# Packed attention into a gated feed-forward: token halves on the partition halves, batch 0 turned by TensorE, attention matmuls beside `pp @ w`, three output buffers

## The chip, the cores and the metric

The kernel runs on one core of a Trainium2 chip. The metric is the device time of one launch in microseconds, from the first to the last instruction of the core with what the launch adds around it. Three runs of the kernel before took 767.19, 770.46 and 770.11 us, a median of 770.11 us. The engines that matter are TensorE (PE; its weight loads are counted apart as PEld), VectorE (DVE), ScalarE (ACT), GpSimd (POOL) and the queue of SyncE (SP), which issues nearly all DMAs.

## What is computed

```python
def sm_attn(qq, kk, vv):                       # softmax attention, scale 1/8
    a = exp(s - max(s)); a = a / (sum(a) + 1e-9)   # s = scale * qq @ kk.T
    return a @ vv
p_packed = sm_attn(p, k, v)                    # 32 packed queries look at 576 tokens
out = sm_attn(q, p_packed, p_packed)           # 576 tokens look at the 32 packed rows
x = out.transpose(0, 2, 1, 3).reshape(8 * 576, 512)
return (x @ w_a) * (x @ w_b) @ w_out           # 512 -> 1536 -> 512
```

There are 8 batches, 8 heads, 576 tokens, a head size of 64 and 32 packed rows. q, k, v and p are float32; the three weight matrices come in as float64 (18.9 MB in all) and are turned into float32 on the chip.

## The kernel before

**The algebra.** `x` is never built. For a batch and a head, `x` is `a2 @ pp`, where `pp` is the packed result (32 rows of 64) and `a2` the second softmax (576 x 32). So `x @ w = a2 @ (pp @ w)`, and with 8 heads of 32 rows the inner dimension is 256, as two tiles of 128. The kernel computes `g = pp @ w` in pieces (`g_tiles`, line 276 on), then `g` times `a2` (`mm1`, `mm1_half`), multiplies the two branches, and multiplies by `w_out` (`mm2_part`). To keep float32 accuracy in fp32r matmuls, operands are split into a high and a low part, and each product is three matmuls (high by high, high by low, low by high).

**A batch on TensorE.** There are 12 steps `ft` of `mm1`, each of two halves of 12 matmuls 128 x 288 (line 303), then the output tiles of `mm2`, each 36 matmuls 128 x 512 (line 329): four tiles after an even batch and five after an odd one. `g_tiles` gives two steps' worth at a time (16 records at line 284, tiles of 64 x 32 of the array), six times a batch; one of the six stands ahead of the last `mm2` tile of the batch before.

**The attention of the next batch** lies between those matmuls. `stage1(b, e)` makes the first softmax of four heads: eight scores matmuls (line 201), maximum and exp, five transposes of `a1` (lines 224 and 225), then 20 small matmuls by v (line 234), scaled into `pp`. `stage2(b, u)` makes the second softmax of one token half: eight matmuls (line 250), a 32 x 32 transpose, maximum, subtraction, exp, sum, scaling, transpose back, and the high and low parts `a2_hi` and `a2_lo`. `turned` transposes p and `pp` on TensorE (line 190) into `pT` and `ppT`. Both stages are generators: each `next` runs one step up to a `yield`.

**What sets the order.** All engines are scheduled by hand. Two strings, `FIRST` and `START`, give the order of loads and of batch 0's attention and weight conversions before the main loop. `PLAN` (and `PLAN_0` during batch 0) says at which slot which step of the next batch is emitted. There is a slot after each half of `mm1` (0 to 23) and after each three `ft` of an `mm2` tile (24 on). `g_tiles` is emitted after slots 1, 5, 9, 13 and 17. In the strings `S` and `r` are steps of stage 1, `s` of stage 2, `T` and `P` the two `turned`, `k` and `q` the turning of loaded k and q, `L..` loads, `g` the first `g_tiles`, and `A`, `B`, `C`, `D` the conversion of one weight piece (high word on ACT, low word on ACT, DVE or POOL, joined on DVE, and for `w_out` the split on ACT and POOL). There are 36 pieces in 12 raw buffers; a new load waits until a `C` has freed one.

**q and k before the change.** Tokens lie along the free dimension and head parity on the two partition halves: rows 64e to 64e+63 hold the 64 features of head 2r+e. `load` (line 107) reads 128-byte runs, eight DMAs of 72 KB for half of a batch's k or q, so that VectorE's 32 x 32 transposes (line 117) finish the turning. In `stage1` all eight scores matmuls of one `e` read the same partition half: two token halves one behind the other on the same 64 rows of the array. In `stage2` both partition halves are used at a time.

**PSUM.** Three pools: `ps_m` (two buffers of two banks: `mm1`, `mm2`), `ps_s` (one of two banks: scores) and `ps_x` (two banks: `g`, transposes, the product with v). An output tile goes through one SBUF buffer `ob`, which also takes each converted `w_out` piece.

Of the kernel before, what the change touches and what calls it, by code (L numbers as in the profile page):

```python
# [19 lines left out]
def tile_packed_attn_gated_ffn(  # L20
# [78 lines left out]
    def load(src, key, b, i, engines=(nc.sync,)):  # L99

        pool = scratch if b == 0 and key == "q" else ld
        t = pool.tile([P, 2, TX, TL], F32, name=f"nat{i}")
        for r in range(2):
            for e in range(E):
                for w in range(2):
                    g = 64 * e + 32 * w
                    engines[w % len(engines)].dma_start(  # L107
                        out=t[g:g + TL, r],
                        in_=src[b, 2 * (2 * i + r) + e, :, TL * w:TL * w + TL].rearrange("(x l) d -> l x d", l=TL))
# [12 lines left out]
    def load_v(b, e):
        t = ld.tile([P, R, NT, D], F32, name="vt") if b or e == 0 else scratch.tile([P, R, NT, D], F32, name="vt1")
        vv = v[b].rearrange("(r e) s d -> e s r d", e=E)[e]
        nc.sync.dma_start(
            out=t[:, :, 0:4, :], in_=vv[0:512].rearrange("(p i) r d -> p r i d", i=4))
# [60 lines left out]
    def turned(dst, src):  # L187

        tp = bank()
        nc.tensor.transpose(tp[:, 0:P], src.rearrange("p e d -> p (e d)"), ident)  # L190
# [4 lines left out]
    def stage1(b, e):  # L195

        rows = slice(64 * e, 64 * e + 64)
        s = bank_pair(b or e == 0)
        for half in range(2):
            for r in range(R):  # L200
                nc.tensor.matmul(  # L201
                    out=s[J * r:J * r + J, half, 0:HS], lhsT=pT[rows, r, :],
                    rhs=xT_cols(b, "k", rows, r, half), start=True, stop=True)
# [13 lines left out]
        a1v = a1[:, 0:512].rearrange("p (t i) -> p i t", i=4)  # L217
        if b == 0 and e:
            pair = bank_pair()
# [3 lines left out]
        for i in range(4):  # L223
            nc.tensor.transpose(tp[:, P * i:P * i + P], a1v[:, i, :], ident)  # L224
# [323 lines left out]
```

## Time and profile before

| | |
|---|---|
| median of three runs | 770.11 us |
| profiled execution | 769.02 us, its span 767.2 us |
| PE busy | 730.9 us (95% of the span) |
| PE in the first 40 us | 14.3 us |
| DVE, ACT, POOL busy | 309.1, 276.6, 205.6 us |
| first `mm1` matmul | at 43.96 us |
| first `mm1` matmul of batch 1 | at 137.60 us |
| first `mm1` matmul of batch 4 | at 411.92 us |
| DMA | 58.03 MB in 180,173 packets, 159,504 of them under 512 B |

The profile gives for each engine the time in which it executed something, in total and in 40 slices; a chain of waits, followed back from the last instruction; groups of instructions by source line; and a timeline by engine. In a timeline row stand the start, the duration, the engine, the source line, the operation with its output and input, and how many instructions were merged. Matmuls overlap, so what a piece of work costs on TensorE is read from the start of its first row to the start of the next piece, and not from its duration.

### The profile page before, as it was taken

The page shows a single profiled execution, that of the slowest core. Times are in us where ns is not written, and L with a number is a line of the kernel's source. Part 1 is how long each engine was busy: PE and PEld are TensorE (multiplying, and loading weights), DVE is VectorE, ACT ScalarE, POOL GpSimd, SP SyncE. Part 2 cuts the span into 40 slices and gives each one's busy share as a digit, 9 for nine tenths or more (in the row PEclk, how much of TensorE's full clock was granted, in tenths as well). Part 3 has the DMA queues.
Part 4 walks back from the last instruction along what each step waited for, and adds up shares of the span by engine and source line. Part 5 has one row for each costly group of instructions (what it writes and reads, how often), then busy time and mean ns, then how long its engine had stood idle before and what let it go on. Part 6 is the DMA issues. An engine that isn't in the chain of part 4 may idle for free.

```text
span 767.2 us, 13460 instructions
## 1 busy us (share of the span) xinstructions
PE 730.9 (95%) x5652; PEld 595.2 (78%) x5652; DVE 309.1 (40%) x482; ACT 276.6 (36%) x487; POOL 205.6 (27%) x151
## 2 busy tenths in 40 slices
PE   1569999999999999999999999999999999999998
PEld 0267777788778888788787887788888788788887
DVE  3589854544405443344504344054420544223200
ACT  2477653543214432244202542144311443224300
POOL 1154654223202241023401233022310224113300
PEclk9979999999999999999999999999999999999999
DMA  9899843423004230234002350043201310100001
GB/s 224 226 316 290 264 102 68 94 64 63 27 28 80 75 51 28 57 69 93 15 28 63 62 94 15 28 80 87 39 28 41 64 32 1 41 15 2 1 27 42
DMA packets 180173, 58.03 MB, mean 76 GB/s; under 512 B 159504, under 2 KB 167952, under 8 KB 180112
## 3 DMA queue, kind: packets, MB, share of 16 engines
q1 hardware_dynamic: 175376, 56.58, 30.0%
q10 hardware_dynamic: 4736, 0.59, 0.5%
q8 instruction: 44, 0.72, 0.4%
q14 instruction: 17, 0.14, 0.1%
HBM read 47.71 MB, written 9.44 MB: 74 GB/s over the span
## 4 chain that ended last, share of the span: by engine, by line
PE 91%; SPq 2%; DVE 2%; DMA 2%; issue 1%; POOL 1%; ACT 1%; DVEq 0%; ACTq 0%; POOLq 0%
PE m L303 40%; PE m L329 39%; PE x L284 6%; PE s L201 2%; SPq L107 2%; PE x L234 1%; PE s L250 1%; PE x L224 1%; DMA nat<-in_k_dram 1%; DMA vt<-in_v_dram 1%; POOL wo L83 1%; POOL h_lo L83 1%; DVE ob L156 0%; DMA nat<-in_q_dram 0%; ACT h_hi L322 0%
## 5 line engine op out<-in xcount | busy, mean ns | idle before, releaser
L329 PE MATMUL m<-wo,h_hi 128*128 128x512 f32 (+1 forms) x888 | 270.6, 387 | 1.7 <-ACT ob L342 1.5
L83 POOL TENSOR_TENSOR h_lo<-asb,h_hi 128x576 fp32r<-128x576 f32 x96 | 138.9, 1447 | 441.8 <-ACT h_hi L322 441.8
L329 PEld LDWEIGHTS m<-wo,h_hi 128*128 128x128 f32 x888 | 162.9, 188 | 46.0 <-ACT ob L342 7.9
L303 PE MATMUL m<-a_hi,ghi 128*128 128x288 f32 x768 | 175.4, 309 | 8.5 <-ACT a_hi L271 8.1
L329 PE MATMUL m<-wo,h_lo 128*128 128x512 f32 (+1 forms) x444 | 170.5, 384 | 0.0
L303 PE MATMUL m<-a_lo,ghi 128*128 128x288 f32 x768 | 164.8, 295 | 0.6 <-DVE a_lo L83 0.6
L303 PEld LDWEIGHTS m<-a_hi,ghi 128*128 128x128 f32 x768 | 121.9, 189 | 52.3 <-issue 34.3
L303 PE MATMUL m<-a_hi,glo 128*128 128x288 f32 x768 | 134.2, 296 | 0.1
L322 ACT CAST h_hi<-asb 128x576 fp32r<-128x576 f32 x96 | 64.8, 675 | 169.6 <-DVE asb L318 169.6
L303 PEld LDWEIGHTS m<-a_lo,ghi 128*128 128x128 f32 x768 | 125.2, 190 | 0.9 <-DVE a_lo L83 0.9
L318 DVE TENSOR_TENSOR asb<-m,asb 128x576 f32<-128x576 f32 x96 | 72.5, 756 | 125.5 <-PE m L303 118.3
L83 DVE TENSOR_TENSOR glo<-x,ghi 128x512 fp32r<-128x512 f32 x96 | 61.7, 684 | 131.4 <-ACT ghi L290 131.3
L303 PEld LDWEIGHTS m<-a_hi,glo 128*128 128x128 f32 x768 | 113.5, 189 | 0.3 <-DVE glo L83 0.3
L329 PEld LDWEIGHTS m<-wo,h_lo 128*128 128x128 f32 x444 | 83.5, 188 | 16.9
L342 ACT COPY ob<-m 128x512 f32<-128x512 f32 x35 | 20.6, 588 | 174.3 <-PE m L329 171.8
L315 ACT COPY asb<-m 128x576 f32<-128x576 f32 x96 | 61.6, 641 | 23.8 <-PE m L303 21.4
L284 PE MATMUL x<-w_ab,ppT 64*32 64x512 f32 x768 | 53.8, 609 | 0.0
L290 ACT CAST ghi<-x 128x512 fp32r<-128x512 f32 x96 | 51.3, 586 | 2.9 <-PE x L284 2.9
L117 DVE STREAM_TRANSPOSE xT<-nat 128x1152 f32<-128x1152 f32 x32 | 43.8, 1370 | 14.4 <-DMA nat<-in_k_dram 10.2
L145 ACT ACTIVATE raw<-raw 128x512 f32<-128x512 f32 x36 | 23.6, 678 | 15.8 <-DMA raw<-in_moe_w_a_dram 12.1
L201 PE MATMUL s<-xT,pT 64*32 64x288 f32 x240 | 19.7, 427 | 7.2 <-DVE pT L191 7.0
L261 ACT ACTIVATE t<-t 128x576 f32<-128x576 f32 x14 | 9.6, 686 | 43.2 <-POOL t L259 43.2
(86 smaller groups left out, 367.2 us busy)
## 6 DMA issues: line engine op xcount, KB each, us to landing
nat<-in_q_dram SPq DMA_DIRECT2D x128, 72.0 KB
nat<-in_k_dram SPq DMA_DIRECT2D x120, 72.0 KB
vt<-in_v_dram SPq DMA_DIRECT2D x16, 512.0 KB
out_dram<-ob SPq DMA_DIRECT2D x31, 256.0 KB
raw<-in_moe_w_a_dram SPq DMA_DIRECT2D x12, 512.0 KB
raw<-in_moe_w_b_dram SPq DMA_DIRECT2D x12, 512.0 KB
raw<-in_moe_w_out_dram SPq DMA_DIRECT2D x12, 512.0 KB
out_dram<-ob SPq DMA_DIRECT2D x10, 128.0 KB
```

Of the source, the lines that this page charges most:

```text
L83: return eng.tensor_tensor(out=dst, in0=src, in1=hi.bitcast(F32), op=ALU.subtract)
L117: nc.vector.transpose(out=xT.rearrange("p r t -> p (r t)"), in_=t.rearrange("p r x d -> p (r x d)"))
L145: nc.scalar.activation(out=high, in_=high, func=AF.Prelu, scale=2.0 ** -112, alpha=-2.0 ** 32)
L201: nc.tensor.matmul(out=s[J * r:J * r + J, half, 0:HS], lhsT=pT[rows, r, :], rhs=xT_cols(b, "k", rows, r, half), start=True, stop=True)
L284: nc.tensor.matmul(out=gps[e][J * r:J * r + J, :], lhsT=ppT[rows, b % 2, r, :], rhs=w_ab[rows, c, r, :], start=True, stop=True)
L290: nc.scalar.copy(out=ghi[:, e], in_=gps[e])
L303: nc.tensor.matmul(out=ps[:, half, 0:HS], lhsT=gt[:, kt, i, :], rhs=at[:, kt, HS * half:HS * half + HS], start=(n == 0), stop=(n == len(st ...
L315: nc.scalar.copy(out=asb, in_=pa[:, :, 0:HS])
L318: nc.vector.tensor_tensor(out=asb, in0=pb[:, :, 0:HS], in1=asb, op=ALU.mult)
L322: nc.scalar.copy(out=hh, in_=flat)
L329: nc.tensor.matmul(out=o[:, cols], lhsT=ht[:, c0:c0 + P], rhs=wt[:, cols], start=(ft == 0 and n == 0), stop=(ft == NFT - 1 and n == 2))
L342: nc.scalar.copy(out=ob, in_=o)
```

## The change

**Layout.** Half of the tokens now lies on each partition half, with all heads along the free dimension: rows 64u to 64u+63 hold the 64 features of token half u. For k the halves are even and odd tokens, for q alternating blocks of 32 tokens. A load of a half batch is four DMAs of 144 KB instead of eight of 72 KB. `stage1` takes one matmul of 288 columns on one partition half and, on the other, 256 and 32 columns (shifted, so that five contiguous chunks of `a1` match v's token order). `stage2(b, e)` now goes by head parity. Because both partition halves need every head of p and `pp`, both are transposed twice, with the two parities exchanged (`turned`, two transposes instead of one; `p_nat` and `pp` have a third column block that repeats the first).

**Batch 0** is loaded by `load_first` in 1 KB runs (512 B for the last 64 tokens), three DMAs each for k and q, and turned by 24 TensorE transposes each (`turn_first`), whose results ACT and DVE copy to `xT`. Its output rows come in another order and are stored in groups of 32 (`store_first`).

**Order.** `FIRST` puts p, k, q and v ahead of all weights; `START`, `PLAN` and `PLAN_0` are new. `stage1` and `stage2` yield once more, right behind their scores matmuls, so that these can be placed alone. `g` of the next batch is a task of the plan now. The product with v and the transposes of `a1` go to `ps_s` from batch 1 on. **Output tiles** go through three buffers (the two of `asb` and one that was named `ob`).

```diff
-    def load(src, key, b, i, engines=(nc.sync,)):
+    def load(src, key, b, i):
+        t = ld.tile([P, R, XH, TL], F32, name=f"nat{i}")
+        rows = src[b, R * i:R * i + R].rearrange("h s d -> (h s) d")
+        rows = rows.rearrange("(y l u) d -> u l y d" if key == "k" else "(y u l) d -> u l y d", u=2, l=TL)
+        for u in range(2):
+            for w in range(2):
+                g = 64 * u + 32 * w
+                nc.sync.dma_start(out=t[g:g + TL].rearrange("l h x d -> l (h x) d"), in_=rows[u][:, :, TL * w:TL * w + TL])
+    def load_first(src, key, part):
+        if part < 2:
+            t = scratch.tile([P, R, 4 * D], F32, name=f"{key}n{part}")
+            nc.sync.dma_start(out=t, in_=src[0, R * part:R * part + R, 0:4 * P, :].rearrange("h (p i) d -> p h (i d)", i=4))
+        else:
+            t = scratch.tile([P, H, 2 * D], F32, name=f"{key}n{part}")
+            nc.sync.dma_start(out=t[0:TR], in_=src[0, :, 4 * P:S, :].rearrange("h (p u) d -> p h (u d)", u=2))
+    def turn_first(key, n):
+        copy = (nc.vector.tensor_copy, nc.scalar.copy)[int(TURN["kq".index(key) * 5 + n])]
+        x = bank_pair()[:, 0, :] if n in (2, 3) else bank()
+        if n < 4:
+            h = 2 * (n % 2)
+            for i in range(4):
+                nc.tensor.transpose(x[:, P * i:P * i + P], firsts[key, n // 2][:, h + i // 2, P * (i % 2):P * (i % 2) + P], ident)
+            copy(out=xTs[0, key][n // 2][:, h:h + 2, 0:2 * P], in_=x.rearrange("p (h t) -> p h t", h=2))
+            return
+        for h in range(H):
+            nc.tensor.transpose(x[:, TR * h:TR * h + TR], firsts[key, 2][0:TR, h, :], ident[0:TR, 0:TR])
...
-        for half in range(2):
+        parts = [(0, 0, 0, HS), (1, TR, 0, 2 * P), (1, 0, 2 * P, TR)]
+        for u, c, t, n in parts:
             for r in range(R):
                 nc.tensor.matmul(
-                    out=s[J * r:J * r + J, half, 0:HS], lhsT=pT[rows, r, :],
-                    rhs=xT_cols(b, "k", rows, r, half), start=True, stop=True)
+                    out=s[J * r:J * r + J, u, c:c + n], lhsT=pT[64 * u:64 * u + 64, u ^ e, r, :],
+                    rhs=xT_cols(b, "k", u, 2 * r + e, slice(t, t + n)), start=True, stop=True)
+        yield
...
+        for i in range(2):
+            nc.tensor.transpose(tp[:, P * i:P * i + P], cols[:, 64 * (i ^ back):64 * (i ^ back) + P], ident)
...
+    def out_tile(i):
+        if i % 3 == 1:
+            return sm.tile([P, DO], F32, name="wo_f32", bufs=1)
+        return sm.tile([P, 2, HS], F32, name="asb").rearrange("p u t -> p (u t)")[:, 0:DO]
...
-    FIRST = ("p0 w1 k0 k1 w1 v0 w1 v1 w1 q0 q1 w1 w1 w1 w1 w1 w1 w1 w1")
+    FIRST = ("p0 k0 k1 k2 q2 q0 v0 q1 v1 w1 w1 w1 w1 w1 w1 w1 w1 w1 w1 w1")
```

**Where it moves instructions.** First the DMA queue of SP at the program's start (`nat` is a loaded k or q half, `kn` and `qn` the new ones, `raw` a weight piece; before, eight more DMAs of k go through ACT's queue, and eight more of q follow the last row). Before:

```order
L133 DMA p_nat<-in_p_dram 128x1x64 x2
L166 DMA raw<-in_moe_w_a_dram 128x2x512
L107 DMA nat_102<-in_k_dram 32x18x32 x4
L107 DMA nat_111<-in_k_dram 32x18x32 x4
L166 DMA raw<-in_moe_w_a_dram 128x2x512
L125 DMA vt<-in_v_dram 128x4x256
L127 DMA vt<-in_v_dram 64x4x64
L166 DMA raw<-in_moe_w_b_dram 128x2x512
L125 DMA vt_127<-in_v_dram 128x4x256
L127 DMA vt_127<-in_v_dram 64x4x64
L166 DMA raw<-in_moe_w_b_dram 128x2x512
L107 DMA nat_132<-in_q_dram 32x18x32 x8
```

With the change:

```order
L177 DMA p_nat<-in_p_dram 128x1x64 x3
L130 DMA kn_101<-in_k_dram 128x4x256
L130 DMA kn_103<-in_k_dram 128x4x256
L134 DMA kn_105<-in_k_dram 32x8x128
L134 DMA qn_107<-in_q_dram 32x8x128
L130 DMA qn_109<-in_q_dram 128x4x256
L165 DMA vt<-in_v_dram 128x4x256
L169 DMA vt<-in_v_dram 32x4x64 x2
L130 DMA qn_115<-in_q_dram 128x4x256
L165 DMA vt_117<-in_v_dram 128x4x256
L169 DMA vt_117<-in_v_dram 32x4x64 x2
L210 DMA raw<-in_moe_w_a_dram 128x2x512 x2
```

The 32 DMAs of k and q became six, and the first weight piece moved from the second place to behind all of k, q and v.

Then TensorE in `mm1`, around the scores of stage 1 (`s<-xT,pT`) and the second `g_tiles` (`x<-w_ab,ppT`) of a batch. Before:

```order
L303 MATMUL m<-a_hi,glo 128x288 x4
L201 MATMUL s<-xT_1451,pT 32x288 x2
L201 MATMUL s<-xT_1469,pT 32x288 x2
L201 MATMUL s<-xT_1451,pT 32x288 x2
L201 MATMUL s<-xT_1469,pT 32x288 x2
L303 MATMUL m<-a_hi,ghi 128x288 x2
```

With the change:

```order
L351 MATMUL m<-a_hi,glo 128x288 x4
L247 MATMUL s<-xT_1413,pT 32x288 x2
L247 MATMUL s<-xT_1423,pT 32x288 x2
L247 MATMUL s<-xT_1413,pT 32x256 x2
L247 MATMUL s<-xT_1423,pT 32x256 x2
L247 MATMUL s<-xT_1413,pT 32x32 x2
L247 MATMUL s<-xT_1423,pT 32x32 x2
L332 MATMUL x<-w_ab,ppT 32x512 x8
L351 MATMUL m<-a_hi,ghi 128x288 x2
```

The scores, which stood alone between two halves of `mm1`, stand right ahead of `g_tiles` now, and have twelve matmuls in place of eight.

Last, TensorE from the end of `mm1` into the first `mm2` tile, around stage 2's matmuls (`xT,ppT`). Before (a second group like the one shown stands three `ft` further on, and `g_tiles` ahead of the last tile):

```order
L303 MATMUL m<-a_hi,glo 128x288 x4
L329 MATMUL m<-wo,h_hi_396 128x512 x2
L329 MATMUL m<-wo,h_lo_397 128x512
L329 MATMUL m<-wo,h_hi_398 128x512 x2
L329 MATMUL m<-wo,h_lo_399 128x512
L329 MATMUL m<-wo,h_hi_400 128x512 x2
L329 MATMUL m<-wo,h_lo_401 128x512
L250 MATMUL s<-xT_1828,ppT 32x288 x4
L250 MATMUL s<-xT_1880,ppT 32x288 x4
L329 MATMUL m<-wo,h_hi_402 128x512 x2
```

With the change:

```order
L351 MATMUL m<-a_hi,glo 128x288 x4
L297 MATMUL s<-xT_1825,ppT 32x288 x4
L297 MATMUL s<-xT_1921,ppT 32x288 x4
L297 MATMUL m<-xT_1825,ppT 32x288 x4
L297 MATMUL m<-xT_1921,ppT 32x288 x4
L332 MATMUL x<-w_ab,ppT 32x512 x8
L377 MATMUL m<-wo,h_hi_477 128x512 x2
```

Both of stage 2's groups and the next batch's first `g_tiles` form one run between `mm1` and `mm2`; before, there were three runs in three places.

More of the change, by code (lines that the diff above doesn't have):

```diff
@@ L97, in tile_packed_attn_gated_ffn @@
     nats, xTs = {}, {}
-    def load(src, key, b, i, engines=(nc.sync,)):
[L101 to L109, printed above, removed]
+    def load(src, key, b, i):
[5 more added lines that the diff above has]
+                g = 64 * u + 32 * w
+                nc.sync.dma_start(
+                    out=t[g:g + TL].rearrange("l h x d -> l (h x) d"), in_=rows[u][:, :, TL * w:TL * w + TL])
         nats[key, b, i] = t
@@ L216, in stage1 @@
         a1T = work(b, f"a1T_{e}", [P, NT, P], "t2")
[L217 to L219 removed]
+        chunks = [P * i + (HS + TR) * u for i in range(2) for u in range(2)]
+        if b or e:
+            pair = bank_pair(b)
             tp, tq = pair[:, 0, :], pair[:, 1, :]
@@ L222, in stage1 @@
             tp, tq = bank(), bank()
-        for i in range(4):
-            nc.tensor.transpose(tp[:, P * i:P * i + P], a1v[:, i, :], ident)
-        nc.tensor.transpose(tq[0:64, 0:P], a1[:, 512:576], ident)
+        for i, c in enumerate(chunks):
+            nc.tensor.transpose(tp[:, P * i:P * i + P], a1[:, c:c + P], ident)
+        nc.tensor.transpose(tq[0:64, 0:P], a1[:, 2 * P:2 * P + 64], ident)
         nc.scalar.copy(out=a1T[:, 0:4, :].rearrange("p i t -> p (i t)"), in_=tp)
@@ L268, in stage2 @@
         yield
-        a2f = work(b, f"a2f_{u}", [P, E, HS], "t2")
-        nc.vector.transpose(out=a2f.rearrange("p e t -> p (e t)"), in_=s2.rearrange("p x j -> p (x j)"))
+        a2f = work(b, f"a2f_{e}", [P, 2, XH, TL], "t2")
+        nc.vector.transpose(out=a2f.rearrange("p u x l -> p (u x l)"), in_=s2.rearrange("p x j -> p (x j)"))
         nc.scalar.copy(out=hi, in_=a2f)
@@ L284, in g_tiles @@
                 nc.tensor.matmul(
-                    out=gps[e][J * r:J * r + J, :], lhsT=ppT[rows, b % 2, r, :], rhs=w_ab[rows, c, r, :],
+                    out=gps[e][J * r:J * r + J, :], lhsT=ppT[rows, 2 * (b % 2), r, :], rhs=w_ab[rows, c, r, :],
                     start=True, stop=True)
@@ L310, in mm1 @@
         if b == 0 and ft == 0:
-            pa, pb = (mm1_half(i, ghi, glo, halves=(0,)) for i in range(2))
+            pa, pb = (mm1_half(i, ghi, glo, kts=(0,)) for i in range(2))
             mm1_half(0, ghi, glo, pa, (1,))
@@ L316, in mm1 @@
         between()
-        pb = mm1_half(1, ghi, glo, pb, (1,) if pb is not None else range(2))
+        pb = mm1_half(1, ghi, glo, pb, (1,) if pb is not None else range(E))
         nc.vector.tensor_tensor(out=asb, in0=pb[:, :, 0:HS], in1=asb, op=ALU.mult)
@@ L371, in emit @@
             elif what == "T":
-                turned(pT, p_nat.pop(b))
+                turned(pT, p_nat.pop(n))
             elif what == "P":
-                turned(ppT[:, b % 2], pp.pop(b))
+                turned(ppT[:, b % 2:b % 2 + 2], pp.pop(b), b % 2)
             elif what in ("k", "q"):
-                turn(what, b, e)
+                turn(what, n, e % 2) if b else turn_first(what, e)
             elif what == "Lk":
```

163 lines of the change are left out of this document (97 added, 66 removed), and 6 rows, old and new, of the table PLAN_0.

## The prediction

> **What bounds the kernel now.** I read the page's busy times and its chain of waits first, then a steady batch by stretches.
>
> ```profile
> PE 730.9 (95%) x5652; PEld 595.2 (78%) x5652; DVE 309.1 (40%) x482; ACT 276.6 (36%) x487; POOL 205.6 (27%) x151
> PE 91%; SPq 2%; DVE 2%; DMA 2%; issue 1%; POOL 1%; ACT 1%; DVEq 0%; ACTq 0%; POOLq 0%
> 60.00:90.00 30.00, 28.94 (x247) 23.43 (x246) 27.38 (x40) 21.72 (x39) 16.51 (x11) 1.00 0.90 274
> 404.00:496.00 92.00, 92.00 (x712) 75.15 (x711) 35.32 (x56) 30.37 (x54) 21.81 (x16) 1.00 0.25 55
> ```
>
> TensorE sets the end: 91% of the chain, and in a stretch as long as a batch it is busy for all 92 us, while DVE, ACT and POOL have 35, 30 and 22 us to do. So what a steady batch saves is what its path on TensorE gets shorter by. Batch 0 is another matter: from 60 to 90 us DVE is busy for 27.4 of 30 us with weight conversions. And TensorE hardly works before 44 us. The timeline and the chain of that start:
>
> ```profile
> 14.10 14.90 SPq L107 DMA_DIRECT2D nat<-in_q_dram  x16
> 19.76 1.13 PE L224 MATMUL x<-ident,a 128*128 128x128 f32 x4 [3.86 <-ACT a L210]
> 23.32 2.83 PE L234 MATMUL x<-vt,a1T 128*32 128x64 f32 x80 [1.15 <-ACT a1T L226]
> 28.51 2.25 DMA nat<-in_q_dram
> 32.27 0.70 PE m L250 x4
> 33.52 0.78 DVE L254 STREAM_TRANSPOSE s<-m 128x576 f32<-128x576 f32 x1 [1.31 <-PE m L250]
> 34.12 1.73 PE L284 MATMUL x<-w_ab,ppT 64*32 64x512 f32 x12
> 34.34 0.75 DVE L256 TENSOR_REDUCE mx<-s 128x18 f32<-128x576 f32 x1
> 43.13 0.65 DVE L156 SCALAR_TENSOR_TENSOR w_ab<-raw 128x512 uint32<-128x512 uint32 x1
> 43.96 0.61 PE L303 MATMUL m<-a_hi,ghi 128*128 128x288 f32 x1 [8.11 <-ACT a_hi L271]
> ```
>
> Sixteen DMAs of q keep SP's queue busy from 14.1 to 29.0 us, the last data land at 30.8, stage 2's scores follow at 32.3, and 10.4 us of vector work lie between their first read (33.5) and the first `mm1` matmul.
>
> **The steady batch.** TensorE costs are read from start to start.
>
> ```profile
> 413.50 0.27 PE L190 MATMUL x<-ident,p_nat 128*128 128x128 f32 x1
> 413.53 0.51 PE L303 MATMUL m<-a_hi,ghi 128*128 128x288 f32 x2
> 415.30 1.09 PE L284 MATMUL x<-w_ab,ppT 64*32 64x512 f32 x16
> 416.32 0.53 PE L303 MATMUL m<-a_hi,ghi 128*128 128x288 f32 x2
> 419.69 1.18 PE L201 MATMUL s<-xT,pT 64*32 64x288 f32 x16
> 420.80 0.40 PE L303 MATMUL m<-a_hi,ghi 128*128 128x288 f32 x1
> 438.96 0.63 PE L224 MATMUL x<-ident,t 128*128 128x128 f32 x4
> 441.24 0.90 PE L234 MATMUL x<-vt,t 128*32 128x64 f32 x40
> 442.07 0.53 PE L303 MATMUL m<-a_hi,ghi 128*128 128x288 f32 x2
> 457.45 0.43 PE L303 MATMUL m<-a_hi,ghi 128*128 128x288 f32 x2
> 459.05 0.43 PE L303 MATMUL m<-a_hi,ghi 128*128 128x288 f32 x2
> 464.40 0.72 PE L250 MATMUL s<-xT,ppT 64*32 64x288 f32 x16
> 465.05 0.72 PE L329 MATMUL m<-wo,h_hi 128*128 128x512 f32 x2
> ```
>
> Stage 1's scores cost 1.11 us (419.69 to 420.80), stage 2's, with as many columns but both partition halves in use, 0.65. The difference of 0.46 is one half's columns: 0.46 and 0.19 of filling and draining make up the 0.65. `g_tiles` costs 1.02 with 512 columns: 224 columns more for 0.37, so 288 stream in 0.48 and about 0.17 are fill, which agrees. A half of `mm1` takes 1.60 (457.45 to 459.05), but the two halves between `g_tiles` and the scores take 3.37 (416.32 to 419.69), 0.17 more than 3.20: each run of small tiles costs 0.17 for going to that shape of the array and back.
>
> (a) *Scores of stage 1.* Twice a set (the attention of one batch) the two halves run side by side. One chain has 288 columns, the other 256 and 32, two records more on the same part of the array. A small record costs 0.083 there (40 records in 0.83 us at line 234, four at a time), so the new price lies between 0.65 and 0.82; I take 0.74, since the two chains overlap at their ends. Saved: 2 x 0.37 = 0.74. If the halves do not run side by side, it is 1.11 and more, and nothing is saved.
>
> (b) *Runs.* Before there are twelve runs of small tiles in a batch: six `g_tiles`, two scores, two products with v, two groups of stage 2. Now both scores and one product with v stand right ahead of a `g_tiles`, and both groups of stage 2 and the next `g_tiles` form one run: seven runs. Five times 0.17 is 0.85.
>
> (c) *Inside a run* a piece can fill while the last drains: four joints with the same shape (two of scores and `g_tiles`, two in the run of three), each up to 0.17. Nothing in a steady batch shows such a joint, so 0 to 0.68; I take 0.50, near the upper end, since 16 records of both partition halves already run without a pause inside `g_tiles`.
>
> (d) *Two more transposes* of p and `pp`: 0.03 from start to start and 0.08 on the next row (0.51 against 0.43), so 0.11 each, 0.22 lost.
>
> A set saves 0.74 + 0.85 + 0.50 - 0.22 = 1.87 us, between 0.6 and 2.5. Batches 1 to 6 each carry one: 11.2 us. The set in batch 0 is placed otherwise: only one of its scores stands at a `g_tiles`, and stage 2 stays apart. 0.74 + 0.17 + 0.12 - 0.22 makes 0.8.
>
> What must keep hiding: ACT beside the longer runs. At slot 5 it has, behind the half that ends, `h_hi`, two copies of `a1T`, two casts of `ghi` and the next `asb` copy.
>
> ```profile
> L322 ACT CAST h_hi<-asb 128x576 fp32r<-128x576 f32 x96 | 64.8, 675 | 169.6 <-DVE asb L318 169.6
> L315 ACT COPY asb<-m 128x576 f32<-128x576 f32 x96 | 61.6, 641 | 23.8 <-PE m L303 21.4
> L290 ACT CAST ghi<-x 128x512 fp32r<-128x512 f32 x96 | 51.3, 586 | 2.9 <-PE x L284 2.9
> 22.70 0.57 ACT L226 COPY a1T<-x 128x512 f32<-128x512 f32 x1
> 23.16 0.26 ACT L227 COPY a1T<-x 64x128 f32<-64x128 f32 x1
> ```
>
> 0.68 + 0.57 + 0.26 + 2 x 0.59 + 0.64 = 3.3 us, begun 0.9 late (the DVE product must end first), so done 4.2 us after that half. TensorE needs the buffer after transposes 0.5, `g` 1.1 and two halves 3.3: 4.9. Slack 0.7, so I cost it at nothing. The loads cost nothing either: DMA's share is 0.25 there, and each k or q half is now issued some 15 slots (over 20 us) ahead of its turn; a later one would stall TensorE only by what exceeds that. v takes four DMAs a half instead of two and batch 0's rows some 14 more in stores, at 0.5 us each on SP's queue, and behind them stand only loads with that lead.
>
> **The start.** Issuing first: three p loads, then five loads of k and q at one 0.5 us each, where 16 took 14.9.
>
> ```profile
> 10.38 0.47 SPq L125 DMA_DIRECT2D vt<-in_v_dram  x1
> 30.00:31.00 1.00, 0.00 (x0) 0.00 (x0) 0.16 (x1) 0.00 (x0) 0.00 (x0) 1.00 0.94 107
> 170.00:171.00 1.00, 1.00 (x19) 0.48 (x4) 1.00 (x2) 0.53 (x1) 0.00 (x0) 1.00 1.06 373
> ```
>
> Bytes in 128-byte runs came at 107 GB/s with the DMA engines 0.94 busy; v's 1 KB runs at 373. So k's 1.18 MB need 3.2 us from about 4.4 and are there by 7.6 to 8, q by 13. Then the chain goes through TensorE, at the start's pace (four transposes 1.13, twice the 0.63 us of a steady batch): k's 16 transposes of full width 4.5 and eight narrow ones about 1, behind the first landing at 6.2 and k's last part: 12.2. One group of q 1.1, scores 1.4: 14.7. DVE maximum 0.9, exp 0.9: 16.8. Both transposes of `a1` with another group of q before them 3.2: 20.2. Products with v 2 x 1.4, two more groups of q 2.2, `ppT` 0.6, the last of q with its copies 1.6: 27.4. Stage 2's scores 1.2: 28.6, where 33.5 stood before. But the vector part grows: between that point and `a2_hi` four `C` conversions of 0.68 now stand in DVE's order, where there was one. I add DVE's list: two transposes, two maxima, one subtraction, two sums with reciprocals, one scaling, four `C`, one transpose, 0.7 to 0.8 each (sums 1.15), 10.4; then `a2_hi` twice and the first `ghi` on ACT, 1.8: first `mm1` matmul at 40.9. That is 3.0 earlier. With some of TensorE's pace regained I take 4.0, from 1 to 7.
>
> ```profile
> 38.00:39.00 1.00, 0.00 (x0) 0.00 (x0) 1.00 (x2) 1.00 (x3) 0.86 (x2) 0.93 1.03 379
> 39.00:40.00 1.00, 0.00 (x0) 0.00 (x0) 0.93 (x4) 1.00 (x3) 1.00 (x1) 0.50 1.06 389
> 48.00:50.00 2.00, 2.00 (x13) 2.00 (x12) 0.79 (x2) 0.52 (x1) 0.00 (x0) 0.72 1.06 389
> ```
>
> Before, the granted clock fell to 0.50 after TensorE had idled from 35.9 us (the row at 34.12), and came back at 49, some 5 us into `mm1`. The gap ahead of `mm1` stays as long (29.6 to 38), so this loss of 2 us stays.
> The Trainium skill, "TensorE: Matmul & The Clock Gate", "What's actually happening", has full rate granted after about 3.4 us of sustained work and half rate after as long an idle window. The fall agrees. By that rule the new start, with transposes back to back from 9 us, would soon run at full pace; the products with v after 3.4 us of nearly unbroken work (19.76 to 23.32) still ran at 2.83 us for 80, where a steady batch takes 0.83 for 40, so this trace does not yet bear it out.
>
> **Batch 0's outputs.** Two waits for `ob` go, since three buffers outlast a store:
>
> ```profile
> 129.28 0.73 PE L329 MATMUL m<-wo,h_hi 128*128 128x512 f32 x2 [0.73 <-ACT ob L342]
> 135.42 0.73 PE L329 MATMUL m<-wo,h_hi 128*128 128x512 f32 x2 [0.75 <-ACT ob L342]
> ```
>
> That saves 1.5. The rest of batch 0, bound partly by conversions, I take as unchanged, with 3 us either way: six `C` lie ahead of `mm1` where five did, and DVE loses batch 0's four q and k transposes and gains five shorter copies.
>
> **Sum.** 769.0 (767.2 of span and 1.8 around it) - 11.2 - 0.8 - 4.0 - 1.5 = 751.5 for an execution like the profiled one. The median of the runs lies 1.1 above that execution, with 3.3 between the runs; I add half: 752.
>
> **Rivals.**
> 1. *TensorE wakes early* in the start: about 12 us of its work there (24 transposes a tensor, products, scores) would halve, some 4.5 us of it on the chain, of which 1 is in the forecast. For it: unbroken work. Against it: the rows above. 752 - 3.5 = 748.5. Chance 0.18.
>    This is what the clock gate page of the Trainium skill, named above, would make of it.
> 2. *The halves do not run side by side and joints give nothing*: (a) and (c) fall out, a set saves 0.6, and 6 x 1.24 + 0.86 is lost: 760. For it: eight records of one half are queued ahead of the other half's. Against it: `g_tiles` keeps both busy. Chance 0.10.
> 3. *Batch 0 gives the start back*: the first weights land behind 3.6 MB (4.4 + 3.6 / 0.373, so at 14 to 16 us, where one weight load went second of all), DVE at 91% cannot deliver `C` earlier, and `mm1` waits ahead of its `g_tiles` for what it began early: 752 + 4 to 6, so 757. For it: 27.4 of 30 us. Against it: the new order has twelve pieces landed before `mm1` needs its fifth. Chance 0.15.
> 4. *Slower*: evictions beside the runs come late. The place is ACT at slots 5, 9 and 17 of six batches, 18 places; the price of a delay d at each is 18 x (d - 0.7). It eats the whole gain of 18 at d = 1.7 us, half as much again as ACT's list; at d = 2.0 the time is 752 + 23 = 775. Against it: ACT is busy a third of the batch. Chance 0.05.
> 5. *The layout does not do what it says*, and TensorE has as much to do: only start and buffers, 764. The matmul rows in the new order speak against it. Chance 0.02.
>
> The forecast has 0.50. Its own range is 747 to 757; with cases 1 to 3 it is 744 to 761. A measurement here can tell about 0.5% from no change, 766.3 to 774.0. Faster: 0.90; within: 0.05; slower: 0.05.
>
> **What would show it.** Batches 1 to 3, 274.3 us before from `mm1` to `mm1`, should take 268.7; the scores row 0.5 to 0.8 from its start to that of `g_tiles`; `mm1` should begin near 40 us, and batch 1's near 131; no wait for `ob` should be left. 272 for the three batches would mean case 2, an early `mm1` with batch 1 still at 135 case 3, and waits of TensorE for ACT in steady batches case 4. A start as late as 44 us, or a steady batch no shorter, would make the prediction wrong.

## The result, and the profile after

| | before | with the change | difference | forecast |
|---|---|---|---|---|
| median | 769.79 us (4 runs, 767.19 to 770.46) | 747.06 us (4 runs, 746.92 to 747.79) | -22.7 | -18.1, to 752 (744 to 761) |
| ratio, 95% interval | | 0.9713 (0.9689 to 0.9736) | | |
| span of the profiled execution | 767.2 | 745.3 | -21.9 | |
| start, up to the first `mm1` | 43.96 | 36.97 | -7.0 | -4.0 |
| batch 0: from there to batch 1's first `mm1` | 93.64 | 92.35 | -1.3 | -2.3 |
| the six batches 1 to 6 | 540.50 | 526.93 | -13.6 | -11.2 |
| batch 7 | 89.1 | 89.05 | 0 | 0 |

The forecast has its sign, its size within 5 us and the order of its parts right; the time lies inside the range. It is 5 us too careful: the steady batches saved 2.4 more than forecast and the start 3.0 more, and batch 0 saved 1.0 less. In the start not the forecast's own case came true but its rival 1, which had a chance of 0.18 (below). Rival 1's 748.5 is 1.4 too slow: the 2.4 of the steady batches less the 1.0 of batch 0.

The page of the changed kernel, its busy times and the engines' shares of the chain of waits:

```profile
PE 719.9 (97%) x5844; PEld 602.9 (81%) x5844; DVE 308.8 (41%) x487; ACT 281.4 (38%) x494; POOL 214.1 (29%) x155
PE 91%; DVE 3%; DMA 1%; POOL 1%; issue 1%; ACT 1%; SPq 0%; DVEq 0%; POOLq 0%; ACTq 0%
```

From the timeline of TensorE, the first `mm1` matmuls of batches 0, 1, 4 and 7 (start, duration, engine, line, what, count):

```profile
36.97 0.54 PE L351 MATMUL m<-a_hi,ghi 128*128 128x288 f32 x2 [0.69 <-ACT ghi L338]
129.32 0.43 PE L351 MATMUL m<-a_hi,ghi 128*128 128x288 f32 x2
396.98 0.42 PE L351 MATMUL m<-a_hi,ghi 128*128 128x288 f32 x2
656.25 0.42 PE L351 MATMUL m<-a_hi,ghi 128*128 128x288 f32 x2
```

TensorE is busy 11 us less and sets the end as before. Batches 1 to 3 take 396.98 - 129.32 = 267.7 us where 268.7 was forecast (274.3 before).

The same timeline at three places of a steady batch that the forecast speaks of: scores and `g_tiles` of stage 1, the product with v and `g_tiles`, and the run of three.

```profile
417.69 0.69 PE L247 MATMUL s<-xT,pT 64*32 64x288 f32 x20
418.23 1.24 PE L332 MATMUL x<-w_ab,ppT 64*32 64x512 f32 x13
419.39 0.53 PE L351 MATMUL m<-a_hi,ghi 128*128 128x288 f32 x2
434.10 0.84 PE L281 MATMUL s<-vt,t 128*32 128x64 f32 x36
434.76 0.24 PE L281 MATMUL s<-vt,t 64*32 64x64 f32 x4
434.82 1.04 PE L332 MATMUL x<-w_ab,ppT 64*32 64x512 f32 x12
435.79 0.53 PE L351 MATMUL m<-a_hi,ghi 128*128 128x288 f32 x2
445.98 0.72 PE L297 MATMUL s<-xT,ppT 64*32 64x288 f32 x16
446.49 0.69 PE L297 MATMUL m<-xT,ppT 64*32 64x288 f32 x16
446.97 1.06 PE L332 MATMUL x<-w_ab,ppT 64*32 64x512 f32 x16
447.97 0.72 PE L377 MATMUL m<-wo,h_hi 128*128 128x512 f32 x2
```

From start to start: scores and `g` 1.70 us, product and `g` 1.69, the run of three 1.99.

The start, from the timeline of all engines:

```profile
9.30 1.03 PE L152 MATMUL x<-ident,kn 32*128 32x32 f32 x8 [1.32 <-DMA kn<-in_k_dram]
10.26 1.11 PE L147 MATMUL x<-ident,kn 128*128 128x128 f32 x4
11.17 1.91 PE L147 MATMUL m<-ident,kn 128*128 128x128 f32 x8
12.88 0.73 PE L147 MATMUL x<-ident,qn 128*128 128x128 f32 x4
13.53 0.77 PE L247 MATMUL s<-xT,pT 64*32 64x288 f32 x10
15.18 0.66 PE L147 MATMUL x<-ident,qn 128*128 128x128 f32 x4
18.56 0.90 PE L281 MATMUL x<-vt,a1T 128*32 128x64 f32 x40
23.61 0.78 DVE L302 STREAM_TRANSPOSE s<-s 128x576 f32<-128x576 f32 x1 [1.09 <-PE s L297]
32.11 2.18 DVE L200 SCALAR_TENSOR_TENSOR w_ab<-raw 128x512 uint32<-128x512 uint32 x2
32.89 3.39 PE L332 MATMUL x<-w_ab,ppT 64*32 64x512 f32 x16 [7.88 <-DVE w_ab L200]
```

Four transposes take 1.11 us at 10.26 and 0.66 at 15.18; 40 records of the product with v take 0.90, where 80 took 2.83 before. The trace's own record of clock changes has the first rise at 13.12 us, 3.8 us after TensorE had begun to work without a pause at 9.30. This is the forecast's rival 1.

### The profile page after: what moved, and what is told of

It reads as the page before. It is cut to its first block, busy times and chain, and to the rows that moved or that the text cites. A ratio compares the mean times of both kernels' runs of the same rounds, so it can differ in the third digit from the quotient of the medians.

```text
span 745.3 us, 13719 instructions
## 1 busy us (share of the span) xinstructions
PE 719.9 (97%) x5844; PEld 602.9 (81%) x5844; DVE 308.8 (41%) x487; ACT 281.4 (38%) x494; POOL 214.1 (29%) x155
## 3 DMA queue, kind: packets, MB, share of 16 engines
HBM read 47.97 MB, written 9.44 MB: 77 GB/s over the span
## 4 chain that ended last, share of the span: by engine, by line
PE 91%; DVE 3%; DMA 1%; POOL 1%; issue 1%; ACT 1%; SPq 0%; DVEq 0%; POOLq 0%; ACTq 0%
PE m L377 40%; PE m L351 39%; PE x L332 6%; PE s L281 1%; PE s L247 1%; DVE w_ab L200 1%; PE s L297 1%; DMA kn<-in_k_dram 1%; PE s L271 1%; POOL wo L86 1%; DMA raw<-in_moe_w_b_dram 1%; DVE wo_f L200 1%; PE x L236 0%; PE m L297 0%; PE m L147 0%
## 5 line engine op out<-in xcount | busy, mean ns | idle before, releaser
L351 PE MATMUL m<-a_hi,ghi 128*128 128x288 f32 x768 | 171.0, 304 | 2.4 <-ACT asb L363 1.7
L351 PEld LDWEIGHTS m<-a_hi,ghi 128*128 128x128 f32 x768 | 122.1, 188 | 39.7 <-issue 16.8
L351 PEld LDWEIGHTS m<-a_lo,ghi 128*128 128x128 f32 x768 | 123.5, 188 | 1.1 <-DVE a_lo L86 1.1
L332 PE MATMUL x<-w_ab,ppT 64*32 64x512 f32 x768 | 57.9, 606 | 7.9 <-DVE w_ab L200 7.9
L412 ACT COPY asb<-m 128x512 f32<-128x512 f32 x24 | 14.1, 587 | 134.2 <-PE m L377 133.4
L119 DVE STREAM_TRANSPOSE xT<-nat 128x1152 f32<-128x1152 f32 x28 | 38.3, 1367 | 0.0
L412 ACT COPY wo_f<-m 128x512 f32<-128x512 f32 x11 | 6.5, 588 | 55.4 <-PE m L377 55.4
L332 PEld LDWEIGHTS x<-w_ab,ppT 64*32 64x32 f32 x768 | 13.6, 106 | 15.9 <-issue 12.3
L194 POOL TENSOR_SCALAR raw<-raw 128x512 uint32<-128x512 uint32 x11 | 23.7, 2157 | 0.9
```

What stands on the lines that cost most here:

```text
L119: nc.vector.transpose(out=xT.rearrange("p h t -> p (h t)"), in_=t.rearrange("p h x d -> p (h x d)"))
L194: (nc.vector if way == 1 else nc.gpsimd).tensor_scalar(out=low, in0=low, scalar1=2.0 ** -29, scalar2=7.0, op0=ALU.mult, op1=ALU.min)
L332: nc.tensor.matmul(out=gps[e][J * r:J * r + J, :], lhsT=ppT[rows, 2 * (b % 2), r, :], rhs=w_ab[rows, c, r, :], start=True, stop=True)
L351: nc.tensor.matmul(out=ps[:, half, 0:HS], lhsT=gt[:, kt, i, :], rhs=at[:, kt, HS * half:HS * half + HS], start=(n == 0 and kt == 0), stop= ...
L412: nc.scalar.copy(out=ob, in_=o)
```

## Experiments

The runs come from three chips, each with the kernel before beside them (medians 769.59 to 770.39 us); the changed kernel itself had 747.06 and, with the last group, 748.21. The lengths of parts come from one profiled execution each; steady batches repeat within 0.02 us, so tenths of a microsecond can be read there, while medians resolve 1 to 2 us.

**Pieces apart.** Each `PLAN` step that now stands beside `g_tiles` is moved away by one slot.

```diff
-    PLAN = (" | S0 | r0 |  | r0 | r0 |  | r0 Lv1 |  | S1 | r1 | q0 Lk2 ...
+    PLAN = ("S0 |  | r0 |  | r0 | r0 |  | r0 Lv1 | S1 |  | r1 | q0 Lk2 ...
-    ... r1 q1 Lk3 |  | r1 Lv2 |  |  | T2 P0 |  |  | s0 s0 s1 g s0 |  | s1 | ...
+    ... r1 q1 Lk3 |  | Lv2 | r1 |  | T2 P0 |  |  | s0 s0 s1 s0 | g | s1 | ...
```

> The changed kernel with, in each of batches 1 to 6's sets, both stage-1 scores one slot earlier, the second product with v one slot later and the next batch's first g_tiles one slot later: four more runs of small tiles a set, and two joints of one shape and one between shapes gone. Theory (a run costs 0.17 us, and a joint inside a run saves up to as much again): 4 x 0.17 to 4 x 0.34 a set, so batches 1 to 3 go from 267.65 us to 269.7 to 271.7, and the median from 747.1 to 751 to 755. Rival (the saving of a set is all in the halves that run side by side, the place of a piece costs nothing): 267.7 and 747.

Measured 758.29 us (before: 770.39). A steady batch rose by 1.02 us (93.0 against 91.9, and 84.8 against 83.8). Rows of its timeline:

```profile
424.43 0.72 PE L247 MATMUL s<-xT,pT 64*32 64x288 f32 x24
425.08 0.53 PE L351 MATMUL m<-a_hi,ghi 128*128 128x288 f32 x2
445.37 0.90 PE L281 MATMUL s<-vt,t 128*32 128x64 f32 x40
446.20 0.53 PE L351 MATMUL m<-a_hi,ghi 128*128 128x288 f32 x2
454.80 0.72 PE L297 MATMUL s<-xT,ppT 64*32 64x288 f32 x16
455.93 0.74 PE L377 MATMUL m<-wo,h_hi 128*128 128x512 f32 x2
458.23 1.09 PE L332 MATMUL x<-w_ab,ppT 64*32 64x512 f32 x16
459.24 0.73 PE L377 MATMUL m<-wo,h_hi 128*128 128x512 f32 x2
```

The theory holds in the steady batches: four more runs cost 1.02, within 0.68 to 1.36. (Four joints are gone, not three as expected: two of scores and `g_tiles`, one in the run of three, one of product and `g_tiles`.) The rows also price each piece alone. Scores alone take 0.65, so 0.65 + 1.02 = 1.67 beside 1.70 together: their joint with `g` saves nothing. The product with v alone takes 0.83, 1.85 with `g` against 1.69: 0.16 saved. Both groups of stage 2 take 1.13 where one takes 0.65, and 1.13 + 1.01 = 2.14 against 1.99 with `g`: 0.17 and 0.15. Beside that, `mm1` runs 0.09 longer ahead of each small run and 0.10 behind it, so four runs and the joints that are gone make 4 x 0.19 + 0.16 + 0.15 - 2 x 0.03 = 1.01: the parts add up to the 1.02.

But the median rose by 11, not by 4 to 8. Batch 1 alone took 96.88 us instead of 91.93. The timeline there (SP's queue, ACT, TensorE):

```profile
129.66 6.73 SPq L111 DMA_DIRECT2D nat<-in_q_dram  x8
136.49 2.42 SPq L402 DMA_DIRECT2D out_dram<-asb  x4
140.30 0.64 ACT L363 COPY asb<-m 128x576 f32<-128x576 f32 x1 [3.27 <-DMA out_dram<-asb]
141.00 0.53 PE L351 MATMUL m<-a_hi,ghi 128*128 128x288 f32 x2 [2.10 <-ACT asb L363]
```

and the stretch behind it (length; busy us of PE, PEld, DVE, ACT and POOL; granted clock; DMA share; GB/s):

```profile
141.00:144.00 3.00, 3.00 (x15) 3.00 (x16) 1.03 (x3) 1.77 (x4) 1.42 (x1) 0.66 0.00 0
```

Batch 0's last store stands behind eight loads of q on SP's queue, and its tile is an `asb` buffer. Here the second step of batch 1 got that buffer: ACT waited 3.3 us for the store, TensorE 2.1, and then it ran part of the next stretch at a granted clock of 0.66: the clock stood at 0.50 for 3.41 us from 141.93, which costs 1.7. The step's 1.0, 2.1 and 1.7 make nearly all of the 4.95 us that batch 1 lost. In the changed kernel the third step seems to get it: its copy starts at 139.4 without a wait, some 2 us after the store's last DMA was issued. The price of sharing the output tiles with `asb` is thus a near miss that the changed kernel happens to avoid.

**The scores twice.** `for u, c, t, n in parts` becomes `parts * (2 if b else 1)`; the second pass writes the same values.

> The changed kernel with the twelve scores matmuls of stage 1 issued twice each from batch 1 on (same outputs written again), 14 groups. Theory (the two token halves run side by side, so a second pass costs one half's columns, 0.48 to 0.55 us): a set +1.0 to 1.1, batches 1 to 3 from 267.65 to 270.6 to 271.0, the median to 753.8 to 755. Rival (they run one behind the other): +0.96 to 1.1 a group, batches 1 to 3 at 273.4 or more, the median at 760 or more.

Measured 755.02 us (the theory had 753.8 to 755), a steady batch +0.98 us, batches 1 to 3 270.6. That is 0.49 for each second pass, the price of one half's 288 columns (0.48). So the two partition halves run side by side; the rival, at +1.92 a batch, is out.

**One output buffer.** `if i % 3 == 1` in `out_tile` becomes `if True`.

> The changed kernel with every output tile in the single buffer that the w_out pieces use too. Theory (two waits for that buffer at batch 0's end, as before the change): +1.5 us between batch 0's and batch 1's first mm1, and up to +5 if batch 0's stores in four DMAs a tile make each wait longer; nothing in steady batches, whose tiles lie 8 us apart; median 748.6 to 752. Rival (the stores were never late any more): no difference, 747.

Measured 751.85 us: batch 0 95.26 instead of 92.35, and batch 1 93.64 instead of 91.93, later ones unchanged. ACT's copies of the output tiles:

```profile
127.00 0.58 ACT L412 COPY wo_f<-m 128x512 f32<-128x512 f32 x1 [2.62 <-DMA out_dram<-wo_f]
130.73 0.59 ACT L412 COPY wo_f<-m 128x512 f32<-128x512 f32 x1 [3.14 <-DMA out_dram<-wo_f]
134.48 0.58 ACT L412 COPY wo_f<-m 128x512 f32<-128x512 f32 x1 [1.63 <-DMA out_dram<-wo_f]
```

Three buffers are worth 4.6 us with the new stores, not the 1.5 of the two waits before: each of batch 0's tiles is stored in four DMAs now, and ACT waits 1.6 to 3.1 us for each of the three that follow. That batch 1 would lose 1.7 as well was not expected; the granted clock was 0.50 there from 132.8 to 136.2 us, behind these waits, and half of 3.4 is 1.7.

**The old start, kept awake.** In the kernel before, 182 transposes of the identity matrix fill most of TensorE's pauses from 5 to 44 us.

```diff
+    def warm(n):
+        x = bank_pair()
+        for _ in range(n):
+            nc.tensor.transpose(x[:, 0, 0:P], ident, ident)
-    START = ("A B k0 A C T0 k1 A B S0 S1 B C ... r1 A r0 B q0 r1 C P0 q1 B s1 s1 A s0 g s0 ...
+    START = ("A B k0 A C T0 W40 k1 A B S0 S1 W28 B C ... r1 A W8 r0 B q0 r1 C P0 W28 q1 B s1 s1 A s0 g W78 s0 ...
```

> The kernel before with idle TensorE filled by transposes of the identity matrix between 5 and 44 us (174 of them, their results are never read), so that its clock is up through the start. Theory (the start before was bound by the issue of q's 16 DMAs and then by vector work, not by TensorE's pace): stage 2's last scores still near 32.3, the first mm1 at 43.3 to 44.0, and only mm1's first 5 us gain by the clock: batch 1's mm1 1.5 to 3 us earlier, median 767 to 768. Rival (TensorE's pace made the old start long): first mm1 at 41 or earlier, median 765 or less.

Measured 767.46 us against 770.39 for the kernel before, a ratio of 0.9961 (0.9947 to 0.9975).

```profile
23.20 0.90 PE L239 MATMUL x<-vt,a1T 128*32 128x64 f32 x40 [1.61 <-ACT a1T L231]
32.05 0.69 PE L255 MATMUL s<-xT,ppT 64*32 64x288 f32 x16
43.47 0.40 PE L308 MATMUL m<-a_hi,ghi 128*128 128x288 f32 x1 [1.20 <-ACT a_hi L276]
```

With nearly all of TensorE's work from 9.5 us on at full pace the first `mm1` moved by 0.5 us, and batch 0 got 2.65 shorter. The old start was bound by q's loads, as forecast: without the new loads, pace is worth almost nothing there. The 2.65 us are about what half pace costs over the first 5 us of `mm1`, which ran at full pace here.

**One pause filled.** The kernel before with only six such transposes, between those of `a1` and the products with v (`r1 A W6 r0`).

> The kernel before with six transposes of the identity matrix in one place alone, the pause of 1.15 us of TensorE between the transposes of a1 and the products with v in the start (22.2 to 23.3 us). Theory (the clock rises after some 3.5 us of work without a pause of about a microsecond; the pause of 1.15 us was what kept the old start at half pace): the products that follow, 80 records, go to full pace within their first microsecond and take 1.7 to 2.1 us instead of 2.83. Rival (it was not the pause): they take 2.8 us again.

One run, 768.28 us. TensorE's rows:

```profile
19.99 1.13 PE L229 MATMUL x<-ident,a 128*128 128x128 f32 x4 [4.48 <-ACT a L215]
22.19 1.49 PE L100 MATMUL m<-ident 128*128 128x128 f32 x6
23.62 2.28 PE L239 MATMUL x<-vt,a1T 128*32 128x64 f32 x80
27.94 0.76 PE L255 MATMUL m<-xT,ppT 64*32 64x288 f32 x8 [0.47 <-DVE ppT L196]
```

The products took 2.28 us instead of 2.83, and the scores behind them 0.76 instead of 1.19: the clock rose during the products. 80 records take 2.83 at half pace and 1.7 at full, so half of them were done at half pace, up to about 25.1 (the trace's record has the rise at 25.02), 5.0 us after 19.99. In the kernel before the products ended at half pace at 26.15. So the pause was what kept the old start at half pace there; my price missed, since the rise came later than 3.5 us. This rests on one execution of each.

**Awake earlier.** In the changed kernel: `START = ("W11 T0 W7 k0 W5 k4 ...`.

> The changed kernel with 23 transposes of the identity matrix put into TensorE's idle time before 9.3 us (11 ahead of p's transposes, 7 and 5 behind them; results never read). Theory (the clock rises after a few us of unbroken work whatever the work is, and TensorE's pace sets the chain from 9.3 us to the first scores at 13.5): the clock is up by 9 us, the first scores at 11.5 to 12.5, the first mm1 at 35.0 to 36.0 instead of 36.97, median 745 to 746. Rival (the loads of k and q, or the copies of the transposes, set that stretch): scores not before 13.2, mm1 at 36.7 or later, median 747.

Measured 747.25 us, its span 743.8 (745.3 for the changed kernel).

```profile
9.38 0.65 PE L157 MATMUL x<-ident,kn 32*128 32x32 f32 x8 [0.36 <-DMA kn<-in_k_dram]
11.99 0.73 PE L252 MATMUL s<-xT,pT 64*32 64x288 f32 x10
35.40 0.85 PE L356 MATMUL m<-a_hi,ghi 128*128 128x288 f32 x2 [0.69 <-ACT ghi L343]
```

From k's last part to the first scores 2.61 us instead of 4.23, the first `mm1` 1.6 earlier, and batch 1's too (127.81): TensorE's pace does set this stretch, and batch 0 did not take it back in this execution. But the median missed its forecast of 745 to 746 and shows no gain: the four runs spread from 745.61 to 749.14, and the profiled one is the fastest of them. What held the others back no trace shows.

**Kept awake behind stage 2's scores.** In the changed kernel `s1 W64 s0` in `START`.

> The changed kernel with 64 transposes of the identity matrix behind stage 2's scores in the start, so that TensorE does not idle from 25 to 32 us. Theory (the half pace behind the gap is paid by the first g_tiles alone, and ACT has the two casts of a2_hi to do meanwhile): the second half of that g_tiles takes 0.5 to 1.0 us instead of 2.0, but the first mm1 moves by 0.3 at most, and the median stays at 746.8 to 747.1. Rival (g_tiles is what the first mm1 waits for): mm1 1 us earlier, at 36.0, median 746.

Measured 748.49 us, 1.4 above the forecast, which is within what medians resolve. The first `g_tiles` ran at full pace (its second half 1.06), yet `mm1` began 22.19 us after the first maximum on DVE, against 22.25. The half pace of that `g_tiles` is hidden, as expected: ACT's casts stand ahead.

**A shorter start.** Three kernels have a new `START`: two weight pieces are converted in idle time ahead of stage 2, and two C's instead of four stand between stage 2's first vector work and its last transpose. The low word of the first piece goes from ACT to POOL (`WAYS`). The second one adds transposes of the identity matrix as above, the third more of them, and one D behind the `g_tiles` that it delayed.

```diff
-    START = ("T0 k0 k4 k1 k3 k2 q0 S0 S1 r0 q1 r1 r1 r0 r0 r1 r0 q2 r1 q3 P0 q4 A s0 A B s0 s0 B s1 s0 B s1 A s1 "
...
+    START = ("W14 T0 W22 k0 W15 k4 k1 k3 k2 q0 S0 S1 r0 q1 r1 r1 r0 r0 r1 A B r0 q2 A B r1 q3 P0 q4 C C s0 A B s0 s0 A B s1 W64 s0 "
+             "A B s1 A s1 s0 B Lp2 A s1 s0 s1 B A B C C s1 s0 C g s1 C Lk2 C C A B Lv2 "
+             "A B A B A B C A B Lk3 C s1")
-    WAYS = ("000000022220202120112012011200110102")
+    WAYS = ("200000002220202120112012011200110102")
-    ... | C S1 A D B | A Lq1 C B B D | ...
+    ... | C S1 A B | D A Lq1 C B B D | ...
```

> The changed kernel with another START: the first two weight pieces are converted (A, B) on ACT and POOL from 19.4 us and joined (C) on DVE at 22.5, in idle time ahead of stage 2's first vector work; stage 2's first transpose back goes ahead of the second sum, two C's behind that sum, and the second a2_lo ahead of the C's of the second g_tiles. Theory (DVE's list sets the time from stage 2's scores to the second g_tiles): first mm1 at 35.0 to 36.0 instead of 36.97, the second g_tiles at 39.5 to 41 instead of 42.76, and as the rest of batch 0 is partly bound by conversions, the median 744.5 to 746. Rival (batch 0 is bound by its conversions and loads later on, and takes back what the start gains): mm1 earlier, batch 1's mm1 still at 129.2 to 129.6, median 747.

> The new START of the kernel with early conversions and both groups of idle-time transposes together. Theory (the gains add up: TensorE's pace ahead of the first scores, DVE's list behind them): first mm1 at 33.5 to 35.0, median 743 to 745. Rival (batch 0 takes it back): median 746.5 to 747.

> The changed kernel itself once more, as the measure for the next one on the same chip: 746.5 to 748.

> The changed kernel with the new START, 64 transposes of the identity matrix in the gap behind stage 2's scores, more of them ahead of k's first transposes (14, 22 and 15, so that no pause over 0.5 us is left even when k lands late), and one D of batch 0 moved behind the g_tiles that it delays (ACT casts a w_out piece there ahead of ghi and asb, and TensorE waits 1.3 us at 82.8). Theory (TensorE's pace ahead of the first scores -1.5, DVE's list -2 up to batch 1, the moved D -1.3): from the first landed part of k to batch 1's mm1 4 to 5 us less, median 742 to 744 where the changed kernel has 747. Rival (spread of the loads and of batch 0 takes it back, as the medians of the separate kernels suggest): within 1 us of the changed kernel.

The first two have medians of 747.16 and 746.90, where 744.5 to 746 and 743 to 745 were expected: no gain that medians resolve. Then, together on one chip, 748.21 (five runs, 747.24 to 750.56) for the changed kernel again and 745.87 (five runs, 745.27 to 746.85) for the third. So the third is 2.3 us faster than the changed kernel, where 3 to 5 were expected. The traces tell where it went; times in us:

| | k's last part there | first scores | first maximum on DVE | first `mm1` | batch 1's `mm1` |
|---|---|---|---|---|---|
| changed kernel | 9.30 | 13.53 | 14.72 | 36.97 | 129.32 |
| the same again | 9.44 | 14.00 | 14.92 | 37.17 | 129.52 |
| awake earlier | 9.38 | 11.99 | 13.14 | 35.40 | 127.81 |
| new START | 11.95 | 16.51 | 17.63 | 39.50 | 131.31 |
| and awake | 10.49 | 14.91 | 15.91 | 37.04 | 128.57 |
| and awake, D moved | 11.85 | 14.64 | 15.59 | 36.72 | 129.04 |

From the first maximum to `mm1` 22.25 us became 21.87, and 21.13 where TensorE stays awake: 0.4 and 1.1 gained where 1 to 2 were expected. But k landed 1.1 to 2.6 us later in all three kernels with the new `START`, and at 9.3 to 9.9 in all seven with the loads of the change and the old one. No load stands elsewhere before 23 us, and k's DMAs were issued at the same time (2.7 to 4.3 us), so what delays them is open. In the second kernel the clock first rose at 14.7, behind pauses of 0.6 and 1.0 for k; in the third, with more transposes, at 5.6. The moved D lost: the wait of 1.3 us for ACT became one of 1.0 for DVE's product and another of 0.7 later, and batch 0 took 92.32, where the second kernel, without that move, took 91.53.

## Why the prediction was right, point by point

- **What bounds the kernel.** Right: what a set lost on TensorE came off the end, six times.
- **(a) Scores side by side.** Right, and better than the 0.74 taken: 0.65 alone, the lower bound, so 2 x 0.46 = 0.92 saved, not 0.74. The three records on one half cost nothing more.
- **(b) Runs.** Right: 0.85 forecast; entering a run costs 0.09 and leaving it 0.10 (start to start around the rows above), 5 x 0.19 = 0.95.
- **(c) Joints.** The sum is about right, the places are not. 0.50 was taken for four joints of one shape; the two of scores and `g_tiles` gave nothing (-0.03 each), the two in the run of three 0.32, and one that was not counted, between the product with v and `g_tiles`, 0.16. Together 0.42. The Trainium skill ("TensorEngine Tiling (Array Packing)", "Key Properties") has the array drain when the tiling mode changes, and not when only the tile does. The trace agrees inside the product with v: its last eight records are 64 x 32 tiles (four of them in the row at 434.76), and the first four of these start 0.17 us after the four before them, where groups of four otherwise follow after 0.06. So its joint with `g_tiles` is of one shape too. It and the joints in the run of three saved 0.15 to 0.17, that of scores and `g_tiles`, also of one shape, nothing. Why is open.
- **(d) Transposes.** Right: T and P take 0.35, 0.2 more than before with the rows behind them.
- These make 2.1 of the 2.26 us that a set saves (13.6 / 6); the other 0.2 has no place that I can show. So the set's 1.87 became 2.26: (a) was too low by 0.18, (b) by 0.10, (c) too high by 0.08.
- **The start** is where a step failed. Piece by piece: the first scores came at 13.5, 0.2 later than computed (12.2 and one group of q, 1.1), though k was there at 9.3 and not at 8; from there to DVE's first read of stage 2 10.1 us passed instead of 15.3; the vector part took 13.4, not 12.3. (Three additions of the forecast are 0.6 too high together: 16.8 should be 16.5, 20.2 be 20.0, 40.9 be 40.8.) So the surplus of 5.2 us lies in one stretch, which was costed at the start's half pace, while an early rise had a chance of 0.18. 3.1 of it lie between the first product with v and stage 2's scores (18.56 to 22.69, 4.1 us against 7.2), where TensorE's work ran at full pace. Another 1.3 lie in the transposes of `a1` (1.9 against 3.2): the group of q that was added there ran ahead of them, in the wait for exp (15.18), which is overlap and not pace.
- **The case against the early rise** was "nearly unbroken work" from 19.76 to 26 at half pace in the old trace. It held a pause of 1.15 us, and filling that pause alone raised the clock. The rule of the Trainium skill ("TensorE: Matmul & The Clock Gate", "What's actually happening"), full rate after about 3.4 us of sustained work in a window that runs freely, fits the runs. In the changed kernel's trace the clock changes at 13.12, 26.77 and 37.02 us, 4 and 3 times 3.41 us apart, and the window that ends at 13.12 is the first one that work fills. In the kernel before, steps of 3.41 back from its rise at 35.45 give a window from 21.80 to 25.21, which holds the pause (22.17 to 23.32); with the pause filled the clock rose at 25.02. The row that was set against the rule did not speak against it.
- **"This loss of 2 us stays"** failed too. The gap ahead of `mm1` did stay and the clock fell. In the profiled execution `g_tiles`, which stands behind the gap now, ran slowly (32.89, hidden behind ACT's casts), and the clock rose at 37.02, with `mm1`. But that was luck: in the same kernel's second profile, with the same `g_tiles`, it rose at 41.4, 4 us into `mm1`. Batch 0 took 92.35 us in both, so the half pace cost nothing there any more.
- **Batch 0.** Waits for `ob` are gone, as forecast. It got 1.3 shorter, not 2.3, although the half pace in its first 5 us, worth about 2.65 in the kernel before, costs nothing any more, because other waits came in its place, from the table of waits of TensorE:

```profile
PE m L351 <- ACT asb L363: 1.7, 2, 1.3
PE m L351 <- DVE glo L86: 1.0, 1, 1.0
PE m L351 <- DVE a_lo L86: 0.9, 1, 0.9
```

  From the first `mm1` to the second `g_tiles` 5.8 us pass, before 6.2. DVE, with its C's, sets that stretch: in the second profile of the same kernel it is 5.8 too, with `mm1` at half pace (rows of its timeline, and a stretch of it with the granted clock, 0.50, ahead of DMA's share).

```profile
37.17 0.85 PE L351 MATMUL m<-a_hi,ghi 128*128 128x288 f32 x2 [0.69 <-ACT ghi L338]
42.97 1.09 PE L332 MATMUL x<-w_ab,ppT 64*32 64x512 f32 x16
38.00:41.00 3.00, 2.52 (x11) 2.17 (x10) 3.00 (x6) 3.00 (x7) 2.84 (x3) 0.50 0.81 274
```

  It is a small form of rival 3, at 2 us and not 5.
- **Rivals.** 2 is excluded by the scores issued twice. 3 did not come about: batch 1's `mm1` began at 129.3, not at 135, and the kernel that woke earlier kept its 1.6 us to the end of its profiled execution, though its median shows no gain. 4 did not come about: no steady batch has a wait of `mm1` or `mm2` for ACT or DVE; the slack of 0.7 itself was not tested. 5 is out: the scores alone take 0.65, not 1.11.

## What to carry to other kernels

Price a piece on TensorE by where it stands: each run of small tiles among matmuls of the full array cost about 0.2 us here (0.09 in, 0.10 out), so small pieces belong beside one another, and matmuls with half the rows belong on both partition halves. Before a stretch is costed at half pace, look for pauses of a microsecond in it, since one of them was enough here to keep the clock down, and a few throwaway matmuls fill it. Then see whether TensorE's pace sets that stretch at all: in the old start it was worth 0.5 us. A buffer that serves both a store and a product ties the product to everything that stands ahead of that store on its queue.
